# Tail rows of W3's sums from DRAM, operand tails in spare partitions, a fourth staging row, and a reordered first group

## The chip, the core and the metric

The kernel runs on one core of one Trainium2 chip. The metric is the device time of one execution in microseconds (us). TensorE (PE) does the matrix products, VectorE (DVE) and ScalarE (ACT) the elementwise work, GpSimd (POOL) a little arithmetic and the transfers that add into their destination, and SyncE (SP) issues all other transfers (DMAs). Each engine takes its instructions in the order in which the program lists them. A tile is a buffer in on-chip memory (SBUF, 128 partitions); matrix products land in PSUM banks, which ACT or DVE must empty before they are used again.

## The reference

Sequence length S = 2048, width D = 576, hidden width F = 4608; everything is float32.

```
xn  = layernorm(x)
A   = x + attention(xn; wqkv) @ wo       # 32 heads of 18; each token sees 8 keys, 2 apart, itself first
h   = gelu(layernorm(xn) @ w1)           # channel quarters of h are shifted by +1, -1, +2, -2 tokens
x1  = xn + shifted(h) @ w2
B   = x1 + gelu(layernorm(x1) @ w3) @ w4
out = A + B
```

The largest part is the last line of B: 576 to 4608 and back for 2048 tokens.

## The kernel before

Every float32 product is made of three products of split operands: an operand is cut into a high part (ACT rounds it, "copy" or "activation") and a low part (DVE subtracts the high part from the original), and high x high, high x low and low x high are summed in PSUM. So each weight and each activation costs one ACT and one DVE instruction per piece before PE may use it.

The stages, in the order of the program and with the stretch of the profiled span that they take:

- **QKV** (to 195 us): tokens in 16 tiles `t` of 128; per tile two halves (`q_half`). `x_stage` normalises ahead, `z_turn` prepares the input of W1. Raw weights pass through a pair of buffers named `raw`.
- **W1, the shift and W2** (to 313.5 us): `mix_tile`, then a loop over 16 token tiles that adds W2's product to Y, takes the layer norm of x1 (`stats`, `n_turn`) and writes the normalised rows, transposed, to DRAM as `xn`. They come back as `x1n[b]`, b = 0 to 3 (512 tokens each), through `get_n` and are split by `split_n` (part 0: a tail and the first two rows of k; part 1: the other two). In the same loop two transfers build `w3t`, a copy of some tail rows of W3 in DRAM.
- **Plain chunks** (313.5 to 515 us): NPL = 4 chunks of 256 hidden columns, each for the four token blocks: 16 units `u`. A unit does two `up` products (28 matrix products in all, 6.4 us of PE) and then the four `down` products of the unit before (W4, 6.3 us).
- **Groups** (515 to 1200 us): the other NWP = 14 column pairs, for two halves `sb` of the tokens: 28 groups `q`. A group computes four up products of two column chunks and two token blocks with seven instead of eight (Winograd's form of Strassen's method): P1 to P7 (`product`), on sums of W3's quarters (`combine`, then `split_a` and `split_s`, tiles `w3a` and `w3s`) and on sums of activations (`sums` builds T1 to T4 in DRAM, `get_op` loads them, `split_op` splits them into `area[sb]`). Eight `down` products D0 to D7 of the group before lie between them, in an order written out by hand (`ORDER`, `ORDERS`); `plan` and `at(item, f)` put the other work behind a named item. K is 288 = 2 x 128 + 32: the tail of 32 rows is stacked three times into 96 partitions (high, low, high) so that one product covers its three terms. `get_op` loads the tail into partitions 0 to 95 and `split_op` makes rows 64 to 95 the low part through a scratch row of Y, chosen by `rtemps`.
- **W3's pairs**: `load_pair(q)` fetches the raw columns of a pair into `w3st` (two 256 KB and four 64 KB transfers on SP) once the last reader of that buffer has let go; `combine` sums them in place on DVE. `split_ws` writes the high parts and subtracts for the low parts; the low part of the tail is made by a POOL transfer that adds raw tail rows onto `w3a[32:64, 0]` from `w3t` in DRAM (line 983) and onto `w3s[32:64, 0]` from `w3st` itself, after `combine` (line 992).
- **Down products**: `down(t)` uses a PSUM bank that `ahead` has opened. For token tiles not in YD a bank is either seeded with Y by ACT (line 849) and copied back by ACT (876), or added by DVE (879). For the ten tiles in YD, ACT copies the bank (873) into a staging row, a row of Y that `EV` names, and POOL adds that row to DRAM (874). The row is free again when that transfer has landed. `EV` goes round: rows 9, 11, 10, 13, 15 from unit 4 on, 9, 11, 10 from unit 13 until group 22.
- **Attention** (unit 2 until group 22) is a generator on DVE; after each item `bg` lets it issue about 1.6 us of work less what the item itself put on DVE (`spent`).
- **Wo** (1215 to the end): the attention's output comes back as `xo[b]`, split by `split_x`, and the products are added to Y and stored.

Of the kernel before, what the change touches and what calls it, by code (L numbers as in the profile page):

```python
# [29 lines left out]
HF = D // 2  # L30
# [27 lines left out]
def fused_block(ctx, tc, x, wqkv, wo, w1, w2, w3, w4, out):  # L58
# [39 lines left out]
    w3t = dram.tile([NWP, 32, 384], F32, name="w3t")  # L98
    yd = {t: dram.tile([128, D], F32, name=f"yd{t}") for t in YD}
# [524 lines left out]
    for t in range(NT):  # L624
# [38 lines left out]
        if t > 13:  # L663
            split_n(1, x1n[1], t - 14)
# [135 lines left out]
    rtemps = [2]  # L800
# [110 lines left out]
    def get_op(sb, k):  # L911
# [6 lines left out]
        for a in range(0, 96, 32):  # L918
            sp.dma_start(dst[a:a + 32, 0, :], src[256:])

    def split_op(sb, k, part=None):
# [6 lines left out]
        if part != 0:  # L928
            spent[0] += 0.7
            rtemps.append(rtemps.pop(0))  # L930
            r = temp(rtemps[-1]).bitcast(F32R)
            if sb:
                dve.tensor_scalar(r[64:96], raw[64:96, 0, :], sg, None, op0=ALU.mult)
# [52 lines left out]
    def split_s(q, steps=(0, 1, 2)):  # L986
        if 0 in steps:
# [4 lines left out]
                 lambda t: pool.dma_start(t, st[32:64, 0], accum_op=ALU.add))  # L992
# [16 lines left out]
    for u, (c, b) in enumerate(units):  # L1009
# [15 lines left out]
        if z == -2:  # L1025
            rtemps[:] = [2, 13, 15]
        r = 0.0 if u < 4 else (RATE[0] if z < -2 else RATE[1]) / 6
        for i in range(C):
# [5 lines left out]
            if (u, i) == (0, 0):  # L1034
                get_n(2, x1n[2])
                load_w3p(1, (0,))
# [7 lines left out]
            if (u, i) in ((1, 0), (2, 1)):  # L1044
                split_n(u + 1, x1n[u + 1], 0, RT)
# [17 lines left out]
        for j, (t, parts) in enumerate(prev):  # L1063
# [8 lines left out]
            if u in (1, 2) and j == 1:  # L1072
                split_n(u + 1, x1n[u + 1], 1, RT)
# [111 lines left out]
    def o_turn(t):  # L1185
# [5 lines left out]
    ORDERS = {0: "P1 P2 D0 P6 P5 P7 D1 D2 P4 D3 P3",  # L1191
              NWP - 1: "P1 D0 P2 P6 P5 P7 D1 P4 P3 D2 D3 D4 D5 D6 D7",
              NWP: "D0 D1 P1 D2 P2 P6 D3 P5 P7 D4 P4 P3 D5 D6 D7"}
    spent[0] = 0.0
    for q in range(NQ):
# [4 lines left out]
        if q == 0:  # L1200
            rtemps[:] = [2]
# [30 lines left out]
        if q == 0:  # L1232
            at("P6", split_op, 0, "T4")
            at("D1", gelu22)
            at("P7", split_a, n, (0, 1))
            at("D1", split_op, 0, "B22")
            at("D1", split_a, n, (2,))
            at("D2", low22)
            at("P3", gelu12)
            at("P3", combine, n)  # L1240
            at("P3", low12)
            at("P3", split_s, n, (0, 1))
            at("P3", split_s, n, (2,))
            at("P3", load_pair, q + 2)
        elif q == NWP - 1:
            rtemps[:] = [2, 13]
# [15 lines left out]
        elif q == NWP:  # L1262
            rtemps[:] = [2]
# [48 lines left out]
        if z < -1 and q + 1 != NWP:  # L1312
            at("D5" if q else "P3", load_w4, NPL + pair(q + 1), 0)
# [14 lines left out]
        for it in ORDERS.get(q, ORDER).split():  # L1328
# [42 lines left out]
            if z < -6 or z == -6 and EV[0]:  # L1371
                bg(1.6 - spent[0], it == "P6" and q != NWP - 1)
# [21 lines left out]
    for j in range(8):  # L1394
# [5 lines left out]
        if j in (0, 2):  # L1400
            split_x(xo[0], j // 2)
# [68 lines left out]
```

## Time and profile before

| | us |
|---|---|
| Median of three runs | 1285.43 (1281.85 to 1287.55) |
| The profiled execution's own time | 1279.72 |
| Its span, first to last instruction | 1277.9 |
| PE busy | 1256.1 |
| DVE busy | 919.6 |
| ACT busy | 742.3 |
| POOL busy | 259.4 |

The granted TensorE clock is 1.0 throughout. How to read the views quoted below: a row of the timeline has start and duration in us, engine, line of the kernel, operation, output <- input, shape and count; square brackets give the idle time of the engine ahead of it and what ended it. "SPq" is SP issuing a transfer, which is not its landing. A row by stretches has the stretch, its length, and then the busy time (and instructions) of PE, its weight loads (PEld), DVE, ACT and POOL, the clock, the busy share of the 16 DMA engines, and GB/s. A row of issues ends with KB and the median time from issue to landing.

### The profile page before, as it was taken

What the parts mean: (1) busy time and instruction counts of PE and PEld (TensorE: products, weight loads), DVE (VectorE), ACT (ScalarE), POOL (GpSimd) and SP (SyncE); (2) the same over time, 40 slices, a digit from 0 to 9 for tenths busy, and PEclk for the clock granted to TensorE, in tenths of its full rate; (3) what the DMA queues carried; (4) which work ended last, traced back from release to release, by engine and by line L of the source; (5) the groups of instructions that cost most, each with busy time, mean ns of one, the idle gap of its engine ahead of it and who ended that gap; (6) DMA issues with size and microseconds to landing.
All of it is one profiled execution on the core that took longest, in us unless ns stands there. A gap on an engine that the chain in (4) does not pass through costs nothing.

```text
span 1277.9 us, 20035 instructions
## 1 busy us (share of the span) xinstructions
PE 1256.1 (98%) x7482; PEld 1149.9 (90%) x7482; DVE 919.6 (72%) x1233; ACT 742.3 (58%) x1181; POOL 259.4 (20%) x374
## 2 busy tenths in 40 slices
PE   8999999999999999999999999998999999999998
PEld 8999998899898998799898989987898898898898
DVE  6455533778548997669899999988999993464341
ACT  3332225525645546777677776856877776677630
POOL 2011100021222121223232222211232222222200
PEclk9999999999999999999999999999999999999999
DMA  7646784346887989588898888696788768899982
GB/s 205 154 123 142 165 172 146 85 121 201 206 227 172 226 155 233 105 208 166 195 239 181 187 179 202 116 277 133 169 172 195 145 106 184 183 212 218 255 254 84
DMA packets 205565, 226.83 MB, mean 177 GB/s; under 512 B 79884, under 2 KB 140652, under 8 KB 205340
## 3 DMA queue, kind: packets, MB, share of 16 engines
q1 hardware_dynamic: 172332, 158.29, 43.5%
q0 software_dynamic: 33136, 67.26, 32.7%
q8 instruction: 59, 0.97, 0.3%
q14 instruction: 38, 0.31, 0.1%
HBM read 127.78 MB, written 107.97 MB: 184 GB/s over the span
## 4 chain that ended last, share of the span: by engine, by line
PE 58%; DMA 5%; DVE 3%; issue 3%; ACT 2%; SPq 1%; POOL 0%; DVEq 0%; POOLq 0%; ACTq 0%
PE ps L868 27%; PE cc L1130 20%; PE p L832 6%; PE ps L215 4%; DMA w3st<-in_B_w_dram 3%; DMA x1n<-td1T 1%; DMA yd<-Y 1%; DMA xt<-td1T 1%; DVE w3st L965 1%; DVE c L826 0%; DVE po L722 0%; DMA xt<-td0T 0%; PE p L1437 0%; POOL yd L874 0%; SPq L957 0%
## 5 line engine op out<-in xcount | busy, mean ns | idle before, releaser
L868 PEld LDWEIGHTS ps<-w,c 128*128 128x128 f32 x3456 | 477.2, 188 | 27.2 <-ACT Y L873 3.8
L868 PE MATMUL ps<-w,c 128*128 128x288 f32 x3456 | 489.4, 295 | 9.0 <-ACT Y L873 3.0
L874 POOL DMA_DIRECT2D yd<-Y x154 | 139.7, 910 | 359.0 <-ACT Y L873 294.5
L826 DVE TENSOR_TENSOR c<-Y,c 128x512 fp32r<-128x512 f32 x144 | 98.7, 687 | 74.4 <-ACT Y L815 73.2
L1130 PE MATMUL cc<-xt,w3s 128*128 128x512 f32 (+1 forms) x588 | 149.3, 393 | 1.5 <-DVE Y L1140 1.5
L873 ACT COPY Y<-ps 128x576 f32<-128x576 f32 x154 | 98.0, 637 | 63.8 <-PE ps L868 51.4
L215 PE MATMUL ps<-WQ,xt 128*128 128x432 f32 x672 | 134.8, 360 | 0.0
L215 PEld LDWEIGHTS ps<-WQ,xt 128*128 128x128 f32 x672 | 125.6, 188 | 5.7
L1130 PEld LDWEIGHTS cc<-xt,w3s 128*128 128x128 f32 (+1 forms) x588 | 107.5, 188 | 22.7 <-DVE Y L1140 1.9
L1130 PE MATMUL cc<-x1n,w3a 128*128 128x512 f32 x392 | 100.2, 394 | 0.3 <-ACT cc L1333 0.3
L876 ACT COPY Y<-ps 128x576 f32<-128x576 f32 x92 | 59.0, 641 | 68.6 <-PE ps L868 67.0
L746 DVE TENSOR_TENSOR po<-q,k 128x1152 f32<-128x1152 f32 (+1 forms) x48 | 84.3, 1756 | 1.2 <-DMA k<-qkvd 0.4
L749 DVE TENSOR_REDUCE L<-po 128x64 f32<-128x1152 f32 (+1 forms) x48 | 84.1, 1751 | 0.8
L122 POOL TENSOR_TENSOR rs<-rs,mhalf 128x1 f32<-128x1 f32 x48 | 30.9, 644 | 258.2 <-DVE rs L121 147.9
L1130 PEld LDWEIGHTS cc<-x1n,w3a 128*128 128x128 f32 x392 | 70.5, 188 | 13.3 <-ACT cc L1333 0.5
L324 ACT COPY stg<-ps 128x864 f32<-128x864 f32 x24 | 21.2, 882 | 102.7 <-PE ps L215 55.8
L1140 DVE TENSOR_TENSOR Y<-cc,Y 128x512 f32<-128x512 f32 x57 | 39.2, 687 | 57.2 <-ACT Y L1136 54.3
L722 DVE TENSOR_TENSOR po<-v,L 128x1152 f32<-128x1152 f32 x56 | 75.7, 1355 | 0.9
L726 DVE TENSOR_TENSOR po<-po 128x1152 f32<-128x1152 f32 x49 | 66.4, 1355 | 0.8
L965 DVE TENSOR_TENSOR w3st<-w3st 128x384 f32<-128x384 f32 x108 | 60.0, 556 | 3.1
L849 ACT COPY ps<-Y 128x576 f32<-128x576 f32 x92 | 59.3, 645 | 4.8 <-DVE Y L879 2.4
L1130 PE MATMUL cc<-xt,w3a 128*128 128x512 f32 (+1 forms) x196 | 51.6, 402 | 3.6 <-ACT Y L1136 3.4
(192 smaller groups left out, 1897.3 us busy)
## 6 DMA issues: line engine op xcount, KB each, us to landing
yd<-Y POOLq DMA_DIRECT2D x156, 288.0 KB, 6.3
Y<-in_B_w_dram SPq DMA_DIRECT2D x31, 576.0 KB, 5.9
w3st<-in_B_w_dram SPq DMA_DIRECT2D x60, 256.0 KB, 7.9
qkvd<-stg SPq DMA_DIRECT2D x24, 432.0 KB, 3.6
yd<-ev POOLq DMA_DIRECT2D x26, 288.0 KB, 6.4
w3st<-in_B_w_dram SPq DMA_DIRECT2D x108, 64.0 KB, 8.1
xd<-st SPq DMA_DIRECT2D x16, 320.0 KB, 6.0
xd<-big SPq DMA_DIRECT2D x16, 320.0 KB, 6.9
```

Of the source, the lines that this page charges most:

```text
L215: pe.matmul(ps[:, h, :n], xs(a), ws(b, h), start=i == 0, stop=i == len(PAIRS) - 1)
L722: dve.tensor_tensor(dst, vv, Lf[:, :, w:w + 1].to_broadcast([128, TPP * GH, HD]), op=ALU.mult)
L726: dve.tensor_tensor(o, o, dst, op=ALU.add)
L746: dve.tensor_tensor(dst, qf[:, None, :].to_broadcast([128, n, TPP * GC]), win, op=ALU.mult)
L749: dve.tensor_reduce(Lw[:, w:w + n, :], dst.rearrange("p w (x d) -> p w x d", d=HD), axis=AX.X, op=ALU.add)
L826: dve.tensor_tensor(h[:, 1, :], g, h[:, 0, :].bitcast(F32), op=ALU.subtract)
L832: pe.matmul(ps, W3[f][:, w, :], x1n[b][:, a, :], start=n == 0, stop=n == len(PAIRS) - 1)
L868: pe.matmul(ps[:, k, :HF], h[:, col], w[:, p, k * HF:(k + 1) * HF], start=n == 0 and not seed, stop=n == len(seq) - 1, skip_group_check=True)
L873: act.copy(e.rearrange("p (h c) -> p h c", h=2), ps[:, :, :HF])
L874: pool.dma_start(yd[t], e, accum_op=ALU.add)
L965: dve.tensor_tensor(st[:, :, o, :], st[:, :, o, :], st[:, :, i, :], op=op)
L1130: pe.matmul(ps, WX[w][:k, v, SLOT[w], :], area[sb][xk][:k, a, :], start=onto is None and i == 0, stop=last and i == len(HALVES) - 1, skip_ ...
```

## The change

- `load_tails` (QKV, t = 8) loads W3's tail rows of all 14 pairs into the `raw` buffer with eight transfers (pairs in four sets of four on 4 x 32 partitions; the last set overlaps); `sum_tails` (t = 10) makes `combine`'s sums of them with four DVE instructions and writes them with four transfers to a new DRAM tensor `w3ts`. `split_s` then adds its tail rows from `w3ts` and not from `w3st`.
- `get_op` loads a fourth copy of the operand tail, into partitions 96 to 127, that no product reads. `split_op` makes the high part of rows 0 to 95 in one ACT instruction, and the low part of rows 64 to 95 from the fourth copy and the high part. The scratch row, its ACT instruction (first half) or DVE instruction (second half), and `rtemps` go.
- The row of Y that this frees, row 2, joins the staging rows from unit 4 on.
- Order of the first group: P4 P3 D3 in place of P4 D3 P3; `gelu22` and the last step of `split_a` go from D1 to D2, `low22` from D2 to P4, and `combine`, `split_s`, the loads of the pair and of W4 from P3 to D3.
- Group 14 (`q == NWP`) calls no attention work behind P1, P2, P6, P5, P7, P4, D2 and D3.
- `split_n` of block 1, part 1, goes from token tile 15 to behind the first `up` of unit 0. In unit 2, part 0 of block 3 goes from behind the second `up` to behind the second `down`, part 1 from there to behind the third.
- After the last group, `split_x(xo[0])` goes from the first and third `down` to the second and fourth.

```diff
+    w3ts = dram.tile([NWP, 32, 512], F32, name="w3ts")
...
+    PER = -(-NWP // 4)
+    first = [min(g * PER, NWP - PER) for g in range(4)]
+    tails = None
+
+    def load_tails():
+        nonlocal tails
+        r = qpool.tile([128, 5 * CG], F32, name="raw", bufs=2)
+        tails = r[:, :512 * PER].rearrange("p (n o c) -> p n o c", n=PER, o=4)
+        for g, p in enumerate(first):
+            for k in range(2):
+                sp.dma_start(tails[32 * g:32 * g + 32, :, 2 * k:2 * k + 2, :]
+                             .rearrange("p n o c -> p n (o c)"),
+                             dram_ap(w3, (256 + HF * k) * F + 256 * (NPL + p),
+                                     [[F, 32], [256, PER], [1, 256]]))
+
+    def sum_tails():
+        for o, i, op in ((1, 0, ALU.subtract), (0, 2, ALU.add), (2, 1, ALU.subtract),
+                         (3, 2, ALU.subtract)):
+            dve.tensor_tensor(tails[:, :, o, :], tails[:, :, o, :], tails[:, :, i, :], op=op)
+        for g, p in enumerate(first):
+            n = g * PER - p
+            sp.dma_start(w3ts[g * PER:p + PER].rearrange("n r c -> r n c"),
+                         tails[32 * g:32 * g + 32, n:].rearrange("p n o c -> p n (o c)"))
...
+                if t == 8:
+                    load_tails()
+                if t == 10:
+                    sum_tails()
...
-        if t > 13:
-            split_n(1, x1n[1], t - 14)
+        if t == 14:
+            split_n(1, x1n[1], 0)
...
-        for a in range(0, 96, 32):
+        for a in range(0, 128, 32):
             sp.dma_start(dst[a:a + 32, 0, :], src[256:])
...
-            rtemps.append(rtemps.pop(0))
-            r = temp(rtemps[-1]).bitcast(F32R)
-            if sb:
-                dve.tensor_scalar(r[64:96], raw[64:96, 0, :], sg, None, op0=ALU.mult)
-            else:
-                act.activation(r[64:96], raw[64:96, 0, :], AF.Identity, scale=sg)
-            act.activation(xt[0:64, 0, :], raw[0:64, 0, :], AF.Identity, scale=sg)
+            act.activation(xt[0:96, 0, :], raw[0:96, 0, :], AF.Identity, scale=sg)
...
-            signed(xt[64:96, 0, :], raw[64:96, 0, :], sg, r[64:96])
+            signed(xt[64:96, 0, :], raw[96:128, 0, :], sg, xt[64:96, 0, :])
...
-                 lambda t: pool.dma_start(t, st[32:64, 0], accum_op=ALU.add))
+                 lambda t: pool.dma_start(t, w3ts[pair(q)].rearrange("p (o c) -> p o c", o=4),
+                                          accum_op=ALU.add))
...
-            EV[0] = (9, 11, 10, 13, 15)
+            EV[0] = (9, 11, 10, 2, 13, 15)
         if z == -3:
-            EV[0] = (9, 11, 10)
...
+            EV[0] = (9, 11, 10, 2)
...
             if (u, i) == (0, 0):
+                split_n(1, x1n[1], 1)
...
-            if (u, i) in ((1, 0), (2, 1)):
-                split_n(u + 1, x1n[u + 1], 0, RT)
+            if (u, i) == (1, 0):
+                split_n(2, x1n[2], 0, RT)
...
-            if u in (1, 2) and j == 1:
-                split_n(u + 1, x1n[u + 1], 1, RT)
+            if (u, j) in ((1, 1), (2, 1), (2, 2)):
+                split_n(u + 1, x1n[u + 1], 1 if u == 1 else j - 1, RT)
...
-    ORDERS = {0: "P1 P2 D0 P6 P5 P7 D1 D2 P4 D3 P3",
+    ORDERS = {0: "P1 P2 D0 P6 P5 P7 D1 D2 P4 P3 D3",
...
+    quiet = ("P1", "P2", "P6", "P5", "P7", "P4", "D2", "D3")
...
-            at("D1", gelu22)
             at("P7", split_a, n, (0, 1))
             at("D1", split_op, 0, "B22")
-            at("D1", split_a, n, (2,))
-            at("D2", low22)
+            at("D2", gelu22)
+            at("D2", split_a, n, (2,))
+            at("P4", low22)
             at("P3", gelu12)
-            at("P3", combine, n)
             at("P3", low12)
-            at("P3", split_s, n, (0, 1))
-            at("P3", split_s, n, (2,))
-            at("P3", load_pair, q + 2)
+            at("D3", combine, n)
+            at("D3", split_s, n, (0, 1))
+            at("D3", split_s, n, (2,))
+            at("D3", load_pair, q + 2)
...
-                bg(1.6 - spent[0], it == "P6" and q != NWP - 1)
+                if q != NWP or it not in quiet:
+                    bg(1.6 - spent[0], it == "P6" and q != NWP - 1)
...
-        if j in (0, 2):
+        if j in (1, 3):
             split_x(xo[0], j // 2)
```

More of the change, by code (lines that the diff above doesn't have):

```diff
@@ L799, in fused_block @@
     RT = temp(2)
-    rtemps = [2]
     evc = [0]
@@ L1021, in fused_block @@
         if u == 4:
-            EV[0] = (9, 11, 10, 13, 15)
+            EV[0] = (9, 11, 10, 2, 13, 15)
         if z == -3:
-            EV[0] = (9, 11, 10)
-        if z == -2:
-            rtemps[:] = [2, 13, 15]
+            EV[0] = (9, 11, 10, 2)
         r = 0.0 if u < 4 else (RATE[0] if z < -2 else RATE[1]) / 6
@@ L1199, in fused_block @@
         cp = ca if q else None
-        if q == 0:
-            rtemps[:] = [2]
         if z == -1:
@@ L1262, in fused_block @@
         elif q == NWP:
-            rtemps[:] = [2]
             at("D0", split_op, 1, "T1", 0)
@@ L1312, in fused_block @@
         if z < -1 and q + 1 != NWP:
-            at("D5" if q else "P3", load_w4, NPL + pair(q + 1), 0)
+            at("D5" if q else "D3", load_w4, NPL + pair(q + 1), 0)
         if 0 < q < 9:
```

1 line of the change is left out of this document (removed).

## The prediction

> **What bounds the kernel.** I read the busy times first, then a table by stretches, then the waits of PE and its timeline, and at each wait the timelines of the engine that ended it.
>
> ```profile
> span 1277.9 us, 20035 instructions
> PE 1256.1 (98%) x7482; PEld 1149.9 (90%) x7482; DVE 919.6 (72%) x1233; ACT 742.3 (58%) x1181; POOL 259.4 (20%) x374
> ```
>
> PE is busy for 1256.1 of 1277.9 us, and the change takes no matrix product away. So it can only win PE's idle time, 21.8 us in all, and only where it works. Columns: stretch, length, busy us of PE, PEld, DVE, ACT, POOL, clock, DMA share, GB/s.
>
> ```profile
> 18.00:313.50 295.50, 295.42 (x1672) 277.62 (x1673) 173.73 (x394) 109.24 (x184) 31.36 (x76) 1.00 0.59 147
> 510.00:560.00 50.00, 47.23 (x275) 41.56 (x275) 29.06 (x38) 37.29 (x58) 11.45 (x14) 1.00 0.60 122
> 560.00:826.00 266.00, 263.23 (x1579) 239.00 (x1578) 250.25 (x258) 197.63 (x306) 72.20 (x85) 1.00 0.85 190
> 826.00:890.00 64.00, 58.67 (x343) 51.73 (x342) 56.29 (x64) 39.37 (x63) 13.64 (x16) 1.00 0.85 198
> 1195.00:1215.30 20.30, 18.25 (x134) 17.61 (x134) 8.26 (x12) 15.59 (x26) 5.57 (x7) 1.00 1.01 251
> ```
>
> Length less PE: 0.08, 2.77, 2.77, 5.33 and 2.05 us idle, 13.0 us in all: 1% is the most that the change could win in these stretches, which hold nearly all of it. The single waits of PE:
>
> ```profile
> 332.71 1.86 PE L868 MATMUL ps<-w,c 128*128 128x288 f32 x12 [1.52 <-ACT ev L873]
> ...
> 535.14 0.80 PE L868 MATMUL ps<-w,c 128*128 128x288 f32 x4 [0.88 <-ACT c L820]
> 537.32 1.32 PE L868 MATMUL ps<-w,c 128*128 128x288 f32 x8 [1.39 <-DVE c L826]
> ...
> 624.88 1.87 PE L1130 MATMUL cc<-xt,w3a 128*128 128x512 f32 x7 [2.25 <-ACT Y L1136]
> ...
> 855.74 1.84 PE L868 MATMUL ps<-w,c 128*128 128x288 f32 x12 [1.47 <-ACT Y L873]
> ...
> 868.20 1.87 PE L1130 MATMUL cc<-x1n,w3s 128*128 128x512 f32 x7 [0.95 <-ACT Y L1136]
> ...
> 872.43 1.88 PE L1130 MATMUL cc<-xt,w3a 128*128 128x512 f32 x7 [0.77 <-ACT Y L1136]
> 875.79 1.88 PE L1130 MATMUL cc<-xt,w3s 128*128 128x512 f32 x7 [1.48 <-DVE Y L1140]
> ...
> 1207.21 8.20 PE L868 MATMUL ps<-w,c 128*128 128x288 f32 x60 [1.53 <-ACT Y L873]
> ```
>
> The profiled execution took 1279.72 us, below all three runs shown (median 1285.43): in those, 5.7 us more went into waits that this trace doesn't show.
>
> **The change part by part.**
>
> *QKV.* Eight loads, four sums, four stores. A 128x512 sum takes 0.69 us (533.73, below), so 2.8 us on DVE, which has 295.5 - 173.7 = 122 us free in that stretch. PE idles there for 0.08 us. Twelve issues of 0.46 us (two in 0.92, row at 611.23 below) put 5.5 us on SP ahead of the stores of Q, K and V, whose four staging buffers cover it. I take 0; without that cover, at most DVE's 2.8 and SP's 5.5.
>
> *Units 0 to 3.* The wait at 332.71 stays: ACT stands there before a load that isn't moved. Part 1 of block 1 changes places with one low part of 0.69 us; PE first wants it in its seventh product: 0, at most +0.7. Block 3 is another matter.
>
> ```profile
> 342.08 0.63 ACT L606 ACTIVATE Y<-x1n 64x512 fp32r<-64x512 f32 x1
> ...
> 344.22 0.62 ACT L873 COPY Y<-ps 128x576 f32<-128x576 f32 x1
> ```
>
> ```profile
> 344.35 1.23 DVE L597 SCALAR_TENSOR_TENSOR x1n<-x1n 128x1024 fp32r<-128x1024 f32 x1 [0.85 <-ACT x1n L609]
> ...
> 347.42 0.82 DVE L201 TENSOR_TENSOR w3s<-w3st,w3s 128x640 fp32r<-128x640 f32 x1
> ```
>
> Now part 0 runs on ACT from 342.08 until the second down's copy takes over at 344.22, 2.2 us. The copy could start when PE has done that down, at 344.0; moved behind it, part 0 runs from 344.6 to 346.9, and its subtraction of 1.23 ends at 348.1. Unit 3 starts at 347.1, as the second unit's last down ends; a product takes 0.23 (seven in 1.61, below), so the third wants that piece at 347.6: 0.5 us of wait. Then DVE has W3's split (0.82, at 347.42 now) and the third down's add (0.75) ahead of part 1, whose first low piece comes at 350.3 for a ninth product due at 349.5: 0.8 more. Nothing covers this, since PE has only this unit to do: +1.3 (0 if ACT is quicker, +2.2 if all that ACT does is seen).
>
> *First group.* 0.88 + 1.39 = 2.27 us of wait for `c12`.
>
> ```profile
> 533.73 0.69 DVE L1140 TENSOR_TENSOR Y<-cc,Y 128x512 f32<-128x512 f32 x1
> 534.34 2.33 DVE L965 TENSOR_TENSOR w3st<-w3st 128x384 f32<-128x384 f32 x4
> ...
> 538.72 0.78 POOL L992 DMA_DIRECT2D w3s<-w3st  x1 [2.97 <-PE ps L868]
> ...
> w3s<-w3st POOLq DMA_DIRECT2D x27, 64.0 KB, 2.5
> ```
>
> The landing of the transfers of line 983, from `w3t` in DRAM:
>
> ```profile
> DMA to landing us min/median/max: 2.4/4.0/8.0
> ```
>
> ```profile
> 540.66 1.77 PE L1130 MATMUL cc<-xt,w3s 128*128 128x512 f32 x7
> 542.27 1.75 PE L868 MATMUL ps<-w,c 128*128 128x288 f32 x12
> 543.86 1.79 PE L1130 MATMUL cc<-xt,w3s 128*128 128x512 f32 x7
> ```
>
> Seven products take 1.61 us, a D 1.59. P3 a D earlier, and `low12` no longer behind `combine` (2.33): D0 of the next group finds its operand, and the wait goes. Late next are the S weights. DVE's addition comes at 533.73 - 1.59 = 532.1; then DVE stands idle for two gelus on ACT (512 columns each, 0.63 as at 342.08) and does `low12` (0.69) before `combine`: 532.1 + 0.69 + 1.3 + 0.69 + 2.33 = 537.1, no earlier than now (536.7). POOL's transfer follows 2.1 behind, as now, at 539.2. With 2.5 to landing, P6's last product goes at 541.7 and P6 ends at 541.9, against 542.3 now. That is -0.4; with the 4.0 of a source in DRAM, +1.1; with `combine` early enough, -2.3. I take 2.5, since only 0.60 of the DMA is busy there (the row of 510 to 560).
> The Trainium skill's page "DMA: Bandwidth & Descriptors" (Anatomy of one DMA) fits 2.0 us plus size over 436 GB/s to a transfer issued from GpSimd: an estimate of 2.15 us for 64 KB, by which this term would be -0.7. The two rows are longer, and the one from DRAM, though smaller, nearly twice as long.
>
> *Groups 1 to 12.* What releases `w3st` for the next load is now the later of that POOL transfer and DVE's subtraction.
>
> ```profile
> 606.80 1.23 DVE L976 TENSOR_TENSOR w3s<-w3st,w3s 128x1024 fp32r<-128x1024 f32 x1
> ...
> 611.23 0.92 SPq L954 DMA_DIRECT2D w3st<-in_B_w_dram  x2
> ...
> 621.01 0.84 ACT L970 CAST w3a<-w3st 128x768 fp32r<-128x768 f32 x1 [4.13 <-DMA w3st<-in_B_w_dram]
> ```
>
> The pair is fetched at 611.23, 3.2 us after the subtraction's end at 608.03. Freed of the transfer it lands 3.2 earlier, ACT's 4.13 us of wait shrinks to 1, and the copy PE waits for at 624.88 is in time: -2.25, and -0.25 for the slower seven behind it (1.87 for 1.62): -2.5. In most groups the subtraction is the later one already; there nothing is won. Between 0 (no transfer is late) and -2.8 (all of the stretch).
>
> *The turn to the second half.*
>
> ```profile
> 826.00:870.00 44.00, 41.58 (x248) 37.33 (x247) 38.50 (x45) 26.71 (x42) 8.86 (x11) 1.00 1.02 261
> ```
>
> ```profile
> 845.98 0.42 DVE L933 TENSOR_SCALAR Y<-x1n 32x512 fp32r<-32x512 f32 x1
> ...
> 873.79 1.35 DVE L749 TENSOR_REDUCE L<-po 128x64 f32<-128x1152 f32 x1
> ```
>
> ```profile
> 853.17 1.06 ACT L927 ACTIVATE xt<-xt 128x1024 fp32r<-128x1024 f32 x1 [0.80 <-DMA xt<-td1T]
> ...
> 855.05 0.64 ACT L873 COPY Y<-ps 128x576 f32<-128x576 f32 x1 [0.83 <-DMA yd<-Y]
> ```
>
> DVE loses seven scratch multiplications, 7 x 0.42 = 2.9 us, and the quiet items two attention pieces of 1.35; what DVE makes PE wait for, 1.48 at 875.79 and most of the 0.7 that the waits shown leave of 5.33, goes: -2.1. Attention runs about as late as before, since the heavy items of that group earned it almost no time. Against it, DVE's tail piece now waits for ACT and the fourth copy, with downs' adds queued behind it, and seven copies of 64 KB (0.46 MB) enter a stretch where the DMA is full: at 261 GB/s, 1.8 us by the last operand, 0.75 by T2, the third. ACT waits for those landings in order and copies PSUM behind them, so its waits (0.95, 0.77) grow by about 1.2. The fourth staging row takes away the 0.83 at 855.05, but the instruction ahead of it waits for T2, which comes 0.75 later: 0, at best -1.5. Together -0.9, between -5.3 (all idle time of the stretch) and +3.2 (seven issues of 0.46, all seen).
> In the first half one ACT instruction of 0.63 goes per operand; PE waits there only for DVE: 0.
>
> *The end.*
>
> ```profile
> 1203.80 0.62 ACT L181 CAST x1n<-x1n 64x512 fp32r<-64x512 f32 x1
> ...
> 1206.52 0.64 ACT L873 COPY Y<-ps 128x576 f32<-128x576 f32 x1 [0.51 <-DMA yd<-Y]
> ```
>
> The second down's copy needs staging row 11, whose transfer landed at 1206.5. Half a `split_x` (1203.80 until ACT's idle 0.51 began at 1206.01, 2.2 us) fills that wait now; moved behind the copy it runs to 1209.3, and the third down's copy and the next bank's seed follow it to 1210.5. PE would have taken that bank at 1208.8: +1.7. If the row is free early, the split no longer holds up the second down's copy and the sum is about 0, at best -1.5. I take +1.7, as the row has it.
>
> Sum: 0 + 1.3 - 0.4 - 2.5 - 0.9 + 1.7 = -0.8 us on 1279.72. Of PE's waits above, those behind a late landing are 1.52 + 2.25 + 1.47 + 0.95 + 0.77 + 1.53 = 8.5; the change relieves 2.25 and part of 1.47, a third. A third of the 5.7 that the median has more is -1.9. So 1285.43 - 2.7 = 1282.7 us.
>
> **The rivals.**
> *All the waits go* (faster). The reordered group, earlier pairs and quiet items take what idle time four stretches have: 2.77 + 2.77 + 5.33 + 2.05 = 12.9, less 1.3 for block 3: -11.6, 1273.8. For it: each part sits at one of the waits. Against: three of them would be followed by the next late thing, as worked out. It decides where landings are no later than here.
> *Operands late at the turn* (slower). ACT takes seven operands in order, each behind its landing; if the extra copy delays each by more than (6.4 + 2.7) / 7 = 1.3 us, the kernel is over 0.5% slower; at 1.7, 1282.7 + 11.9 = 1294.6. For it: the DMA is full from 826 to 870, and ACT waits at 853.17 already. Against: the copies add 0.46 MB to the stretch's 11.5 (44 us by 261 GB/s), 4%.
> The Trainium skill, "DMA: Bandwidth & Descriptors" (Issuing engines are not separate DMA queues), says that transfers of all issuers run on the same 16 DMA engines; by that rule SP's copies also slow POOL's, and the full DMA of this stretch speaks for it.
> *Tail rows from DRAM too late in each group* (slower). P6 reads them in its last product.
>
> ```profile
> 605.42 0.78 POOL L992 DMA_DIRECT2D w3s<-w3st  x1 [4.87 <-ACT w3s L972]
> ...
> 612.84 1.77 PE L1130 MATMUL cc<-xt,w3s 128*128 128x512 f32 x7
> ```
>
> That is 612.84 + 1.4 - 605.42 = 8.8 us after the issue. The transfers from `w3t` take 4.0, 8.0 at most. At 9.2 in 26 groups it costs 26 x 0.4 = 10.4 us: 1293.1.
> *Nothing is released earlier.* If the subtraction ends last in all groups, the 2.5 and the 1.9 fall away: 1287.1, no change.
>
> **How the numbers follow.** 0.5%, about what a measurement of this kernel tells from no change, is 6.4 us: 1279.0 to 1291.9. Forecast 0.36 and nothing released 0.08: 0.44 for no change. All the waits go: 0.33, as the slower runs have more waits to lose. Late operands 0.15, late tail rows 0.08: 0.23 slower. The forecast's own range is 1279 to 1288. For 8 in 10 the range reaches to 1272, past the faster rival, and to 1294, short of the late operands alone.
>
> **What would show it.** Right: no wait near 535, P6 of group 1 waiting for `w3s` instead; the pair's load right at the subtraction's end in each group; nothing released by DVE at the turn; a wait of 0.5 to 1.3 us early in unit 3; a wait at the fifth down after the last group. Wrong: landings at the turn over 1.3 us later, tail rows over 8.8 us after their issue, or DVE behind on attention near group 22.

## The result, and the profile after

| | before | changed |
|---|---|---|
| Median | 1283.37 us (11 runs, 1281.85 to 1287.55) | 1290.09 us (11 runs, 1287.12 to 1295.07) |
| Ratio | | 1.0052, 95% interval 1.0036 to 1.0067 |
| Profiled execution, own time | 1279.72 us | 1287.12 us |
| Granted TensorE clock, mean over the runs | 0.997 (83 runs in all, 0.993 to 1.000) | 0.9955 (11 runs) |

The change makes the kernel slower by 0.52%, 6.7 us. The page of the changed kernel:

```profile
span 1285.3 us, 20052 instructions
PE 1258.8 (98%) x7482; PEld 1152.0 (90%) x7482; DVE 920.0 (72%) x1230; ACT 736.5 (57%) x1174; POOL 259.4 (20%) x374
```

Lines have moved: products are at L1152, downs at L896, the copy for P2 at L1352, `combine` at L987, `split_ws` at L992 to L998, the copies out of PSUM at L901 and L1158. PE's waits in the timeline of the changed kernel (the rows with brackets that answer to those of before, and the product behind the longest one):

```profile
331.94 1.85 PE L896 MATMUL ps<-w,c 128*128 128x288 f32 x12 [0.41 <-ACT ev L901]
347.58 1.65 PE L860 MATMUL p<-x1n,w3a 128*128 128x512 f32 x6 [0.52 <-DVE x1n L626]
349.64 3.68 PE L860 MATMUL p<-x1n,w3a 128*128 128x512 f32 x15 [0.41 <-DVE x1n L626]
...
535.59 0.80 PE L896 MATMUL ps<-w,c 128*128 128x288 f32 x4 [0.44 <-ACT c L848]
536.98 1.32 PE L896 MATMUL ps<-w,c 128*128 128x288 f32 x8 [0.59 <-DVE c L854]
541.41 3.35 PE L1152 MATMUL cc<-x1n,w3a 128*128 128x512 f32 x7 [3.11 <-ACT cc L1352]
544.56 2.88 PE L1152 MATMUL cc<-xt,w3s 128*128 128x512 f32 x7
...
629.86 1.88 PE L1152 MATMUL cc<-xt,w3a 128*128 128x512 f32 x7 [2.21 <-ACT Y L1158]
...
752.87 1.88 PE L1152 MATMUL cc<-xt,w3a 128*128 128x512 f32 x7 [1.68 <-ACT Y L1158]
...
862.96 2.08 PE L896 MATMUL ps<-w,c 128*128 128x288 f32 x12 [1.88 <-ACT Y L901]
...
1207.54 6.78 PE L896 MATMUL ps<-w,c 128*128 128x288 f32 x48 [0.70 <-ACT ps L877]
1215.90 6.61 PE L896 MATMUL ps<-w,c 128*128 128x288 f32 x48 [1.59 <-ACT ps L877]
```

P2 of group 1 (541.41) waits 3.11 us for ACT, and seven products that take 1.61 us elsewhere then take 3.15 (541.41 to 544.56). The changed kernel in windows of 3.41 us around that place (columns as in the prediction):

```profile
536.72:540.13 3.41, 1.32 (x8) 1.09 (x8) 2.35 (x5) 0.93 (x2) 0.88 (x1) 1.00 0.48 47
540.13:543.55 3.42, 2.14 (x5) 1.75 (x6) 1.92 (x2) 3.39 (x7) 0.78 (x1) 0.50 0.46 68
543.55:546.96 3.41, 3.41 (x9) 2.64 (x9) 0.69 (x1) 1.09 (x3) 0.00 (x0) 0.50 0.99 272
546.96:550.37 3.41, 3.41 (x21) 3.07 (x21) 0.00 (x0) 1.88 (x4) 0.21 (x1) 1.00 0.32 122
```

The granted clock is 0.50 for two windows. Nine matrix products start in 3.41 us of full PE work, where the next window has 21. Such a window also stands at 864.40, behind the wait of 862.96. In the profiled execution of before there is none up to the last matrix product.

I matched the 7482 matrix products of the two profiled executions by their order and followed how far the changed kernel runs behind. Both executions are faster than their medians, by 3.7 and 3.0 us, so the table shows where the time goes in these two, and not the average:

| stretch | predicted, us | in the traces, us |
|---|---|---|
| QKV to W2 | 0 | 0.0 |
| units 0 to 3 | +1.3 | +0.8 (332: -1.1; unit 3: +1.6; rest +0.3) |
| units 4 to 15 | 0 | +0.5 |
| first group, to P6 of group 1 | -0.4 | +3.8 (1.1 in waits, 2.7 in half clock) |
| groups 1 to 12 | -2.5 | +1.4 |
| turn to the second half | -0.9 | +0.6 (waits -1.0, half clock +1.6) |
| rest of the groups, end | +1.7 | +0.1 |
| sum | -0.8 | +7.1 |

Half clock is counted by the starts: from 541.41 to 547.28 P2 and P6, seven matrix products each, take 5.87 us in place of 2 x 1.61. The +1.4 of groups 1 to 12 is nearly all one wait, the 1.68 at 752.87.

### The profile page after: what moved, and what is told of

The parts are those of the page before. It is cut to its first block, busy times and chain, and to the rows that moved or that the text cites. A ratio compares the mean times of both kernels' runs of the same rounds, so it can differ in the third digit from the quotient of the medians.

```text
span 1285.3 us, 20052 instructions
## 1 busy us (share of the span) xinstructions
PE 1258.8 (98%) x7482; PEld 1152.0 (90%) x7482; DVE 920.0 (72%) x1230; ACT 736.5 (57%) x1174; POOL 259.4 (20%) x374
## 4 chain that ended last, share of the span: by engine, by line
PE 56%; DMA 6%; issue 3%; ACT 3%; DVE 2%; SPq 1%; POOL 0%; DVEq 0%; ACTq 0%; POOLq 0%
PE ps L896 26%; PE cc L1152 20%; PE p L860 5%; PE ps L216 4%; DMA w3st<-in_B_w_dram 3%; DMA x1n<-td1T 1%; DMA xt<-td1T 1%; DMA x1n<-xn 1%; DMA yd<-Y 1%; DVE w3st L987 0%; DMA xt<-xn 0%; ACT Y L901 0%; ACT xt L955 0%; PE p L1457 0%; DVE po L775 0%
## 5 line engine op out<-in xcount | busy, mean ns | idle before, releaser
L896 PEld LDWEIGHTS ps<-w,c 128*128 128x128 f32 x3456 | 477.4, 188 | 26.7 <-ACT ps L877 4.7
L896 PE MATMUL ps<-w,c 128*128 128x288 f32 x3456 | 489.4, 295 | 8.6 <-ACT ps L877 3.8
L1152 PE MATMUL cc<-xt,w3s 128*128 128x512 f32 (+1 forms) x588 | 150.3, 395 | 0.0
L901 ACT COPY Y<-ps 128x576 f32<-128x576 f32 x154 | 98.0, 637 | 65.7 <-PE ps L896 58.9
L1152 PEld LDWEIGHTS cc<-xt,w3s 128*128 128x128 f32 (+1 forms) x588 | 108.7, 190 | 21.3
L1152 PE MATMUL cc<-x1n,w3a 128*128 128x512 f32 x392 | 102.8, 403 | 3.1 <-ACT cc L1352 3.1
L1152 PEld LDWEIGHTS cc<-x1n,w3a 128*128 128x128 f32 x392 | 72.4, 193 | 16.2 <-ACT cc L1352 3.3
L987 DVE TENSOR_TENSOR w3st<-w3st 128x384 f32<-128x384 f32 x108 | 60.0, 556 | 3.1
L1152 PE MATMUL cc<-xt,w3a 128*128 128x512 f32 (+1 forms) x196 | 51.6, 402 | 6.0 <-ACT Y L1158 5.9
```

The costliest lines, as they stand in the source:

```text
L896: pe.matmul(ps[:, k, :HF], h[:, col], w[:, p, k * HF:(k + 1) * HF], start=n == 0 and not seed, stop=n == len(seq) - 1, skip_group_check=True)
L901: act.copy(e.rearrange("p (h c) -> p h c", h=2), ps[:, :, :HF])
L987: dve.tensor_tensor(st[:, :, o, :], st[:, :, o, :], st[:, :, i, :], op=op)
L1152: pe.matmul(ps, WX[w][:k, v, SLOT[w], :], area[sb][xk][:k, a, :], start=onto is None and i == 0, stop=last and i == len(HALVES) - 1, skip_ ...
```

## The experiments

Theory A: the first group's new order puts the copy for P2 behind `split_s` on ACT, and the pause brings the half clock. Rival B: the operands' extra loads cost the time. Theory D, formed on the way: the clock is halved for one window of 3.41 us when PE has been idle for more than about half of the window before; the windows run on their own, whatever the kernel does.

| run | median us | ratio to before, 95% | mean clock |
|---|---|---|---|
| changed, old first group | 1286.66 | 1.0026 (1.0012 to 1.0039) | 0.9970 |
| before, new first group | 1286.47 | 1.0025 (1.0008 to 1.0043) | 0.9964 |
| changed, old block 3 | 1287.85 | 1.0035 (1.0023 to 1.0048) | 0.9962 |
| changed, copy ahead of `split_s` | 1289.64 | 1.0049 (1.0034 to 1.0064) | 0.9972 |
| changed, both old | 1285.43 | 1.0010 (0.9993 to 1.0026) | 0.9965 |
| before, operands' tails only | 1283.35 | 1.0002 (0.9988 to 1.0015) | 0.9971 |
| before, `split_a` later | 1281.57 | 0.9992 (0.9976 to 1.0007) | 0.9976 |
| before, pauses of 1.5 us | 1301.61 | 1.0137 (1.0112 to 1.0163) | 0.9975 |
| before, pauses of 2.7 us | 1318.03 | 1.0265 (1.0226 to 1.0305) | 0.9945 |
| long pauses taken away | 1278.22 | 0.9965 (0.9951 to 0.9979) | 0.9988 |
| the same, turn one item later | 1277.69 | 0.9952 (0.9934 to 0.9971) | 0.9987 |
| the same, T1 behind P1's copy | 1280.98 | 0.9983 (0.9966 to 1.0001) | 0.9972 |

**The first group's order, taken back and alone.** The first kernel has all of the old order and plan, of which the cut shows the main lines; the second has the new ones on the kernel before.

```diff
-    ORDERS = {0: "P1 P2 D0 P6 P5 P7 D1 D2 P4 P3 D3",
+    ORDERS = {0: "P1 P2 D0 P6 P5 P7 D1 D2 P4 D3 P3",
...
-            at("P4", low22)
+            at("D2", low22)
...
+            at("P3", combine, n)
             at("P3", low12)
-            at("D3", combine, n)
```

> The changed kernel with the first group's order and plan put back as they were before (D3 ahead of P3, combine ahead of low12, the pair's and W4's loads behind P3); everything else of the change stays. Theory A (the first group's new order puts the copy for P2 of group 1 behind split_s on ACT, PE stands still for 3.1 us in one piece, and the granted clock is halved for 6.8 us after it): the wait of 3.11 before P2 goes, the two waits of D3/D0 come back (0.88 + 1.39), the clock is 1.00 in 540 to 548, and the kernel gains the 3.8 us that this place cost: 1286.3, ratio to before 1.002. Theory B (the copies and loads of the operands' fourth quarter, or the staging row, cost the time, in the second half of the kernel): no gain, 1290 and 1.005. Theory C (the half clock has nothing to do with the order): the wait goes, the half clock stays, gain about 1.3.

> The kernel before with only the first group's order and plan as in the change (P3 ahead of D3, low12 ahead of combine, split_s and the loads behind D3). Theory A: a wait of about 3 us before P2 of group 1 with the half clock behind it, +3.8 us: 1287.2, ratio 1.003. Theory B: within 0.5 us of before, 1283 to 1284. If the order is harmful only together with the rest of the change (whose ACT work in this group is shorter by 0.65 per operand), it is between.

Taken back, it wins 3.4 us (1290.09 to 1286.66; 3.8 expected); alone on the kernel before, it loses 0.25%, 3.2 us, with 1 outside the interval. B would have given 0 in both. The order and the plan were moved together, so these runs don't say what each line of the plan is worth. PE's timeline of the kernel before with the new order, and then its ACT:

```profile
541.30 3.21 PE L1130 MATMUL cc<-x1n,w3a 128*128 128x512 f32 x7 [3.10 <-ACT cc L1333]
```

```profile
539.10 1.04 ACT L970 CAST w3s<-w3st 128x1024 fp32r<-128x1024 f32 x1 [2.48 <-DVE w3st L965]
540.05 0.72 ACT L972 ACTIVATE w3s<-w3st,kv 96x512 fp32r<-96x512 f32 x1
540.67 0.57 ACT L1333 COPY cc<-cc 128x512 f32<-128x512 f32 x1
```

ACT stands for 2.48 us at `split_s`, which waits for `combine` on DVE; the copy for P2 comes 1.6 us behind that. In the kernel before it stood behind `split_s` too, but PE spent that time waiting in D0 for `low12`, and P2 itself waited only 0.31 (a row of the kernel before):

```profile
538.95 1.87 PE L1130 MATMUL cc<-x1n,w3a 128*128 128x512 f32 x7 [0.31 <-ACT cc L1333]
```

These were two waits at once, of which the change removed one.

What theory A said of the clock did not hold. With the old order the clock was still 0.50 for a window at 540.53, behind 1.86 us of idle time in the window before, and at 629.27, where P4 of group 4 had waited 2.27 us (windows of the changed kernel with the old order):

```profile
625.86:629.27 3.41, 1.14 (x8) 0.86 (x7) 1.51 (x3) 2.95 (x6) 0.77 (x1) 1.00 0.61 114
629.27:632.68 3.41, 3.41 (x12) 2.85 (x11) 3.31 (x6) 1.34 (x3) 0.89 (x1) 0.50 0.46 39
```

The same wait was 2.25 in the profiled execution of before and 2.21 in the changed kernel's, without half clock: there its idle time lay in two windows (1.44 and 0.82, 1.24 and 0.97), here in one. So the half clock at a place is not tied to an edit, and executions of one kernel differ in it too, as the clocks of the 83 runs of before show (0.993 to 1.000).

**Block 3.**

```diff
-            if (u, i) == (1, 0):
-                split_n(2, x1n[2], 0, RT)
+            if (u, i) in ((1, 0), (2, 1)):
+                split_n(u + 1, x1n[u + 1], 0, RT)
...
-            if (u, j) in ((1, 1), (2, 1), (2, 2)):
-                split_n(u + 1, x1n[u + 1], 1 if u == 1 else j - 1, RT)
+            if u in (1, 2) and j == 1:
+                split_n(u + 1, x1n[u + 1], 1, RT)
```

> The changed kernel with block 3's two parts of split_n put back: part 0 behind the second product of unit 2, part 1 behind its second down. My sum of the prediction: the waits at the start of unit 3 (0.52 and 0.41 in the trace of the changed kernel, 1.56 by the starts of its products) go, and nothing else changes: 1288.5, ratio 1.004. Rival: what goes there comes back at unit 3's end or at the next wait: 1290.

The median falls by 2.2 us where 1.6 was expected; the intervals of the two ratios overlap, so the times alone don't show it. In this run's own profile the two waits are gone, but a down ahead of unit 3 waited 1.11 us for ACT in their place, as the rival has it. With both edits back (the run after next), PE waits for nothing between 335 and 356. The moved parts cost 1.6 us there by the starts, in the changed kernel's trace and in that of the run with the old first group.

**The copy ahead of `split_s`.** `s_now` makes the products read the pair's S weights from there on.

```diff
...
-            at("D3", split_s, n, (0, 1))
-            at("D3", split_s, n, (2,))
...
+        if q == 1:
+            plan["P1"][:0] = [lambda: split_s(1, (0, 1)), lambda: split_s(1, (2,)), s_now]
```

> The changed kernel with split_s of the first group's next pair moved from D3 to behind P1 of group 1, so that the copy for P2 stands ahead of it on ACT; combine stays where the change puts it. If the queue on ACT is the cause of the 3.1 us (theory A), P2 starts with D0's end and waits for nothing; the S weights are then ready about 1 us later than now, since ACT has the two gelus of c21 first, and P6 waits 2 to 3 us for them: the wait moves by one product. The time stays within 1 us of 1290 if the half clock follows the moved wait, and falls by 2.6 to about 1287 if the wait there stays too short for it. Rival (the wait is DVE's own, for low12 and combine): P2 waits as before.

PE's timeline:

```profile
540.13 1.79 PE L1152 MATMUL cc<-x1n,w3a 128*128 128x512 f32 x7
542.30 0.50 PE L1152 MATMUL cc<-xt,w3s 128*128 128x512 f32 x1 [0.39 <-ACT w3s L992]
543.56 1.42 PE L1152 MATMUL cc<-xt,w3s 128*128 128x512 f32 x5 [0.76 <-DVE w3s L998]
546.24 0.77 PE L1152 MATMUL cc<-xt,w3s 96*128 96x512 f32 x1 [1.25 <-DMA w3s<-w3ts]
```

P2 waits for nothing; P6 waits 0.39 + 0.76 + 1.25 = 2.4. The windows of 3.41 us behind it:

```profile
542.63:546.04 3.41, 1.60 (x6) 0.86 (x5) 1.57 (x2) 2.43 (x5) 0.78 (x1) 1.00 0.40 87
546.04:549.45 3.41, 3.21 (x13) 3.15 (x14) 0.00 (x0) 0.59 (x1) 0.00 (x0) 0.50 0.99 288
```

The median is 1289.64, as expected for the case that the half clock follows. The queue on ACT was the cause of P2's wait, and behind it the S weights are late anyhow. Short waits in one window bring the half clock like one long wait: the window to 546.04 has 1.81 us of idle (3.41 - 1.60), the next has 0.50.

**Both put back, and the operands' part alone.** The first has both edits above. The second is the kernel before with `get_op`'s fourth copy, `split_op` and the staging row of the change.

> The changed kernel with both put back: the first group's order and plan, and block 3's two parts of split_n. What is left of the change is the sums from DRAM, the fourth copy of the operands' tails with its plain split, the staging row, the quiet items and the two moved split_x. If the two edits add up (first group 3.4 us by the medians, block 3 2.3 us), 1284.4, ratio to before 1.001, and the rest of the change is worth nothing. If the rest costs or gains something of its own that the two hid, 1 us or more away from that.

> The kernel before with only the operands' part of the change: the fourth copy of each tail, the plain split of the tails through it, and staging row 2 in both lists. By the run with both other edits put back (ratio 1.001), it is worth nothing: 1283 to 1285. If the fourth copy's loads make the operands land later at the turn, PE's wait at the last group of the first half (1.47 in the trace of before) is longer, with half clock behind it when it passes 1.7 us: 1285 to 1287. If the saved work on DVE counts, the wait of 1.48 at 875.79 goes: 1281 to 1282.

The two edits account for the loss as far as these runs can tell: what is left of the change is 0.10% slower, with 1 inside the interval (its median is 1.0 us above the 1284.4 of the sum, its ratio as expected), and the operands' part alone cannot be told from nothing. Rival B falls.

**Pauses of a chosen length.** The second kernel has 7 in place of 5.

```diff
-                    act.copy(cb, ca)
+                    for _ in range(5 if q in range(NWP + 2, NQ - 1) else 1):
+                        act.copy(cb, ca)
```

> The kernel before with ACT's copy for P2 done five times over in 11 groups of the second half (the same values each time), so that PE gets 11 pauses of about 1.1 us, one in a group (four more copies at 0.49 us, less the 0.82 us that the first one ends early). Theory D (the granted clock is halved for the next 3.41 us whenever PE is idle for more than about half of a 3.41 us window that runs on its own; in the profiles so far every one of 15 windows with 1.76 us of idle or more was followed by half clock, and none with 1.59 or less): no half clock after these pauses, time 1283.2 + 12.5 = 1295.7. Theory E (any pause can bring the half clock, by chance): some of them are followed by half clock, and the time is above 1298.

> As the kernel with five copies, but with seven, so that each of the 11 pauses lasts about 2.1 us. Theory D: a pause of 2.1 us puts more than 1.7 us into one window of 3.41 us in about 2.1/3.41 = 62% of cases, so about 7 of the 11 are followed by half clock, each at 1.7 us: 1283.2 + 23.3 + 11.9 = 1318.4, where the pauses alone make 1306.5. The Trainium skill (TensorE: Matmul & The Clock Gate, Part 1) states that the clock falls after an idle window of about 3.4 us and advises against idle gaps over about 3 us; by that none of these pauses is followed by half clock, and the time is 1306.5.

There are two runs of each kernel. The pauses came out longer: 15.2 us in 11 with five copies (1.48 at most), 28.4 with seven (2.68 at most). So the time of the first, 1301.61, missed D's 1295.7 and lies where E put it, above 1298, but the longer pauses alone bring it there; what speaks for D is its clock. That the second came within 0.4 us of D's 1318.4 is luck: its pauses were longer and its half-clock windows fewer than in that sum. The first kernel's stretch, then windows of the second around the pauses ahead of 917.47, 946.27 and 974.83:

```profile
890.00:1200.00 310.00, 294.19 (x1734) 262.87 (x1733) 220.77 (x263) 231.69 (x373) 75.89 (x89) 1.00 0.80 166
```

```profile
914.97:918.38 3.41, 0.91 (x4) 0.79 (x5) 0.64 (x1) 3.28 (x8) 0.24 (x1) 1.00 1.07 259
918.38:921.80 3.42, 3.42 (x10) 2.64 (x9) 3.31 (x3) 2.30 (x5) 0.00 (x0) 0.50 1.10 231
942.28:945.69 3.41, 1.31 (x10) 1.07 (x9) 0.17 (x1) 3.22 (x7) 0.89 (x2) 1.00 1.06 258
945.69:949.11 3.42, 2.84 (x7) 2.26 (x8) 1.85 (x2) 2.71 (x5) 0.00 (x0) 0.50 1.11 265
...
973.00:976.41 3.41, 1.58 (x7) 1.34 (x8) 0.59 (x1) 3.31 (x7) 0.00 (x0) 1.00 1.06 240
976.41:979.83 3.42, 3.42 (x22) 3.09 (x21) 3.39 (x3) 2.19 (x4) 0.00 (x0) 1.00 1.09 243
```

None of the short pauses brought the half clock (1.00); of the long ones 4 of 11 did, fewer than the 7 expected. (The other run of this kernel has a mean clock of 0.998 where this one has 0.991, so it had fewer still.) In the three shown it goes by how much of the pause lies in one window: 2.50 and 2.10 us of idle were followed by 0.50, 1.83 (3.41 - 1.58) was not, though the pause was 2.68 as well. Starts of P2, same kernel:

```profile
917.47 2.58 PE L1130 MATMUL cc<-x1n,w3a 128*128 128x512 f32 x7 [2.68 <-ACT cc L1334]
946.27 3.17 PE L1130 MATMUL cc<-x1n,w3a 128*128 128x512 f32 x7 [2.68 <-ACT cc L1334]
974.83 1.87 PE L1130 MATMUL cc<-x1n,w3a 128*128 128x512 f32 x7 [2.68 <-ACT cc L1334]
1002.08 1.89 PE L1130 MATMUL cc<-x1n,w3a 128*128 128x512 f32 x7 [2.39 <-ACT cc L1334]
```

Without half clock a group takes 27.25 us (974.83 to 1002.08), which is eight windows, so the following pauses fall at nearly the same place of a window, which fits that it is 4 and not 7. With it a group takes 28.80 (917.47 to 946.27) or 28.56 (946.27 to 974.83): a half-clock window costs 1.55 us here, or 1.31 where the pause itself fills 0.58 of it (3.42 - 2.84).

**The wait of group 4.** On the kernel before:

```diff
-            at("P5" if q < NWP else "D2", split_a, n, (0, 1))
-            at("D2" if q < NWP else "P7", split_a, n, (2,))
+            at("P7" if q < NWP else "D2", split_a, n, (0, 1))
+            at("D3" if q < NWP else "P7", split_a, n, (2,))
```

> The kernel before with split_a of a first-half group behind P7 instead of P5, and its subtraction behind D3 instead of D2, so that ACT's wait for the pair's load stands behind the copy of cc that P4 needs; the load itself is issued where it was. If ACT's wait for the landing is what holds P4 of group 4 (2.25 at 624.88), and the landing, not the issue, is late there: the wait goes, and with it the half clock that a pause of 2.25 us brings in about two thirds of executions, 2.3 + 1.1 = 3.4 us: 1280, ratio 0.997. Rival: what stands behind it on ACT next (D3's copy) makes PE wait instead: within 1 us of 1283.5.

P4 of group 4 no longer waits:

```profile
622.80 1.79 PE L1130 MATMUL cc<-xt,w3a 128*128 128x512 f32 x7
```

The median falls by 1.5 us of the 3.4 expected, and the interval holds 1: not shown as a gain. In this execution PE's waits for ACT's copies of L873 had grown to 6.7 us in four, where the profiled execution of before has 3.0 in two. The waits of PE from 300 to 1230 us (in all, times, longest), with `split_a` later:

```profile
PE ps L868 <- ACT Y L873: 6.7, 4, 2.9
```

**The long pauses taken away.** The changed kernel with block 3 and `split_a` as in the two diffs above, `split_x(xo[0])` copied on DVE, and:

```diff
+              1: "P1 D0 P2 D1 D2 P6 P5 P7 D3 P4 D4 P3 D5 D6 D7",
...
-            at("P4", low22)
             at("P3", gelu12)
+            at("P3", low22)
             at("P3", low12)
             at("D3", combine, n)
-            at("D3", split_s, n, (0, 1))
-            at("D3", split_s, n, (2,))
-            at("D3", load_pair, q + 2)
...
+            plan["D0"] = [lambda: split_s(1, (0, 1)), lambda: split_s(1, (2,)), s_now, lambda: load_pair(2)] + plan.get("D0", [])
```

The last line is for q = 1. The run with the turn moved came first, then the one with T1 behind P1's copy, then the one with the turn as it was:

> A version meant to take PE's longest pauses away, from the changed kernel: block 3 as before; the first group's order as changed, but low22 behind the sum of P3, the next pair's split_s and load behind D0 of group 1 (after the copy for P2), and D1 and D2 of group 1 ahead of P6; split_a of a group in the first half behind P7 instead of P5 (so that ACT's wait for the pair's load stands behind the copy that P4 needs); all of the turn's split_op one item later, so that T2's late landing does not stand ahead of D6's copy; the copies of split_x for the first block on DVE. By the waits of the changed kernel's trace: first group -4 (0.44 + 0.59 + 3.11), group 4 and the like -4 (2.2 + 1.7 + 0.5), turn -1.5, end -1.6, block 3 -1.5, and with no pause over 1.7 us left the half clock of 5.9 us a run on average falls to about 1: some 13 to 15 us below 1290, so 1276, ratio to before 0.994. Rival: the waits come back at the next item, as after the move of split_s: 1283 or more.

> The version with the long pauses taken away, with one difference: at the turn T1's split stands behind P1's copy for P2, and T3, T4 and B22 follow one item later. In the version before it PE waited 2.40 for that copy, which stood on ACT behind T1's landing, with 3.41 us of half clock after it. If the wait goes, 2.4 us and the half clock go: 1274 to 1275, ratio to before 0.993. If it moves to the next item (D2's copy, or P5 for T1), 1277 to 1278 again.

> The version with the long pauses taken away, with the turn left as in the changed kernel (T2's split behind D6, and so on). In the trace of the version with the turn's splits one item later, the stretch from 826 to 890 gained nothing net against the changed kernel: the wait for D6's copy went, one of 2.40 for P1's copy came, and the half clock stayed. By that this version takes the same time, 1278, ratio to before 0.995 to 0.996, and what beats the kernel before is the first group, the later split_a, split_x on DVE and block 3. If the turn's shift did the work after all: 1280 or more.

PE's timeline of the version with the turn one item later, first group:

```profile
532.32 1.79 PE L1156 MATMUL cc<-x1n,w3a 128*128 128x512 f32 x7
533.94 1.86 PE L900 MATMUL ps<-w,c 128*128 128x288 f32 x12
535.64 1.78 PE L1156 MATMUL cc<-x1n,w3a 128*128 128x512 f32 x7
537.26 3.34 PE L900 MATMUL ps<-w,c 128*128 128x288 f32 x24
540.44 1.56 PE L1156 MATMUL cc<-xt,w3s 128*128 128x512 f32 x6
542.42 2.10 PE L1156 MATMUL cc<-xt,w3s 96*128 96x512 f32 x8 [0.43 <-DMA w3s<-w3ts]
```

P1, D0, P2, D1 and D2 follow each other without a wait, and P6 waits 0.43: the 4.14 us that PE waits here in the changed kernel became 0.43. This version beats both kernels, 0.48% under before (1277.69 where 1276 was expected); with the turn left alone it is 0.35%, 4.5 us. The two intervals overlap, so the turn's shift is not shown to do anything. The mean clock rises from 0.997 to 0.999. Moving T1 behind P1's copy handed the wait on, and at a higher price than either of its forecasts: 1280.98, where `B22` came late for P3 by 3.42 us. Which of the other moves wins how much was not tested one by one.

## Why the prediction was wrong

It forecast 1282.7 us, 2.7 below before, and no change as the likeliest; measured are 1290.09 and a loss clear of noise. That lies inside the wide range of 1272 to 1294 and outside the forecast's own, 1279 to 1288.

- **First group, -0.4: the step that failed.** "P3 a D earlier, ... D0 of the next group finds its operand" was right: 0.88 + 1.39 became 0.44 + 0.59. "Late next are the S weights" looked at P6 and at POOL's transfer and left out what else stands on ACT behind `split_s`: the copy for P2, one product earlier. In the kernel before that copy ended 2.2 us behind `combine` (538.90 against 536.67); with the prediction's own 537.1 for `combine`, P2 starts at 539.3 and P6, 3.3 us after that as before, ends at 542.7, which is +0.4 and not -0.4. `combine` was mis-sized as well. "DVE's addition comes at ... 532.1" did not happen:

```profile
533.58 0.69 DVE L854 TENSOR_TENSOR c<-Y,c 128x512 fp32r<-128x512 f32 x1 [1.07 <-ACT Y L849]
534.19 0.69 DVE L1162 TENSOR_TENSOR Y<-cc,Y 128x512 f32<-128x512 f32 x1
536.23 0.69 DVE L854 TENSOR_TENSOR c<-Y,c 128x512 fp32r<-128x512 f32 x1 [1.36 <-ACT Y L849]
536.84 2.33 DVE L987 TENSOR_TENSOR w3st<-w3st 128x384 f32<-128x384 f32 x4
```

  `low22`, which the change moves behind P4, stands ahead of the addition on DVE and waits for its gelu. This kernel ran 1.2 us behind in this group before any wait (P4 at 528.54 against 527.34); with that taken off, the addition came 0.9 us later than I put it, and so did `combine`'s end, 539.2 where 537.1 was forecast. The largest part, 2.7 us of half clock behind the pause, was in no term of the sum. Measured in place of -0.4: +3.8 us in the trace, +3.4 by the run with the old order.
- **The clock, left out.** I gave the 5.7 us that the median had more than the profile to "waits that this trace doesn't show" and relieved a third of them. Over 83 runs of the kernel before, the mean granted clock is 0.997; the time times what is missing to 1 is 4.0 us. The profiled execution at 1.000 was a lucky one; 3 of the 83 reach that. For the changed kernel the same product is 5.9 us: 2 of its 6.7 us.
- **Block 3, +1.3: right.** Two waits, of 0.52 and 0.41 where 0.5 and 0.8 were forecast, and 1.6 in the trace by the starts.
- **Groups 1 to 12, -2.5: failed.** The pair is fetched right at the subtraction's end, as I said. The wait is still there. DVE, SP and ACT of the changed kernel:

```profile
611.83 1.22 DVE L998 TENSOR_TENSOR w3s<-w3st,w3s 128x1024 fp32r<-128x1024 f32 x1
```

```profile
613.11 0.98 SPq L976 DMA_DIRECT2D w3st<-in_B_w_dram  x2
```

```profile
626.01 0.84 ACT L992 CAST w3a<-w3st 128x768 fp32r<-128x768 f32 x1 [4.12 <-DMA w3st<-in_B_w_dram]
```

  From issue to use are 12.9 us where they were 9.8 (611.23 to 621.01). "Freed of the transfer it lands 3.2 earlier" took the landing to follow the issue; it did not. The kernel ran 5.0 us behind here, so ACT got the pair at the same place of the program as before (621.01 + 5.0). Between issue and use the DMA engines are full in both kernels, and not at the 0.85 of the whole stretch (before, then the changed kernel; a packet counts where it starts, so a share can pass 1):

```profile
611.23:621.01 9.78, 9.78 (x56) 8.57 (x54) 9.50 (x9) 3.77 (x7) 1.75 (x2) 1.00 1.19 313
```

```profile
613.11:626.01 12.90, 12.90 (x73) 11.39 (x72) 12.58 (x11) 5.89 (x11) 3.22 (x4) 1.00 1.11 297
```

  So the pair seems to have stood behind other transfers for as much longer as it was issued earlier. That is argued from these rows; no run tests it.
- **Turn, -0.9: right for the waits** (DVE's 1.48 at 875.79 went; -1.0 in all by the starts), and 1.6 us of half clock, behind 1.88 us of waiting for D6's copy, took it back.
- **End, +1.7: half right.** The fifth down waits 1.59, but the 1.53 ahead of the fourth went for it (the 0.70 at 1207.54 stands where before has a wait of 0.53), and the sum is 0.1. The prediction named this case, "about 0", and took the other.
- **Rivals.** The landings of the transfers from `w3ts` in the changed kernel:

```profile
DMA to landing us min/median/max: 2.4/2.6/5.7
```

  They stay far from 8.8, and "tail rows too late" falls. "Operands late at the turn" falls by the run with the operands' part alone. The time of "tail rows too late", 1293.1, is off by as much (3.0 us) as that of "nothing is released earlier", 1287.1, which comes nearest in kind, for another reason: the pair's load is earlier, and its landing isn't.

## What to carry to other kernels

When a reordering takes one of two waits away that ran side by side, list what stands in each engine's queue behind the second one: here a copy of 0.57 us behind a split decided it. Count pauses of PE not only by their length: short ones cost their length, those that leave PE idle for over half of a 3.41 us window cost another 1.3 to 1.6 us in these traces, so two pauses of 1.3 us well apart should be cheaper than one of 2.6. One profiled execution shows only one throw of this; the mean clock of all runs shows what a kernel pays on average.

## What the runs showed of the hardware

Within the matrix work, half clock came only in whole windows of 3.41 us (or two in a row), and all of them in one execution start at a multiple of 3.413 us from each other, wherever the pause lies. Over the 14 profiles, windows at full clock by PE's idle time in them, and how many were followed by half clock:

```
idle in the window, us    windows    followed by clock 0.50
1.0 to 1.6                     70                         0
1.6 to 1.86                    12                         7
1.86 and more                  26                        26
```

So the limit is near half of the window, 1.7 us; PE's ends are modelled in a trace, which may be why it isn't sharper. A pause of 2.2 us may or may not do it, by where it falls: P4's wait of group 4 was followed by half clock in seven profiles, where 1.96 to 2.29 us of idle time lay in one window, and not in three (before, changed, and changed with the old block 3), where two windows shared it: 1.44 and 0.82, 1.24 and 0.97, 0.97 and 1.24. The Trainium skill (TensorE: Matmul & The Clock Gate, Part 1) describes the free-running window of 3413 ns, which the records show, and asks for an idle window of about 3.4 us before the clock falls; here 1.9 us of idle within a window sufficed each time. A window at half clock was followed by a second one in three cases, after 1.28 (the changed kernel's), 1.78 and 1.78 us of idle in it, and never after 0.58 or less; so less idle time than 1.7 us may keep the clock down, but where that limit lies is open.
